# Gated mix of attention and a dense layer on one Trainium2 core: some of VectorE's SBUF-only work handed to GpSimd, W2 loaded in pieces, wider margins behind transfers

## The chip, the cores and the metric

The kernel runs on one core of one Trainium2 chip. The metric is the device time of one execution in microseconds (us), the median of several runs. Lower is better.

## The reference

Softmax attention with 32 heads of width 20 over 2048 positions, and a dense layer with the activation h * tanh(softplus(h)), both from the same x, mixed by a gate per position. Inputs and output are bf16.

```python
def _A_ref(x, wqkv, wo):              # x (1, 2048, 640), wqkv (640, 1920), wo (640, 640)
    H = 32; Dh = 20
    q, k, v = ...                     # (x @ wqkv) split into heads
    scores = jnp.einsum("bhqd,bhkd->bhqk", q, k) * Dh ** -0.5
    o = jnp.einsum("bhqk,bhkd->bhqd", softmax(scores), v)
    return o.reshape(B, S, D) @ wo    # heads side by side

def _B_ref(x, w1, b1, w2):            # w1 (640, 1536), w2 (1536, 640)
    h = x @ w1 + b1
    return (h * jnp.tanh(softplus(h))) @ w2

x = A_x
g = sigmoid((x * gate_w).sum(-1, keepdims=True))
out = g * _A_ref(x, A_wqkv, A_wo) + (1 - g) * _B_ref(x, B_w1, B_b1, B_w2)
```

## The kernel before

**Tiling.** The 2048 queries are four chunks c of 512 columns, the 32 heads eight groups g of four. Within a group each head j has its own 32 partitions of KT and QT, so that four heads' products run beside each other in TensorE's array. The unit of work is a score block (c, g, kt, j): 128 keys by 512 queries of one head, 4 x 8 x 16 x 4 = 2048 of them. TensorE writes a block's scores transposed (keys on partitions) to a PSUM bank (L1149), something takes the exponential, and TensorE multiplies by V with a column of ones in front (L1385), so that row 0 of each head's output O is the sum that normalises it. O of a group gathers in one PSUM bank, ACC.

**Two ways for the exponential.** ScalarE takes most blocks, two or three banks in one activation, into the ring ETS (emit_e, L1176). The others go through VectorE, four heads of one (c, g, kt) as a *tile*: each block is evicted from PSUM as a 16-bit integer, scale times score plus an offset, whose bits read as float16 are about the exponential (emit_x, L1234). To smooth the error, two shifted copies of the tile are made by adding a constant to the integers (piece, L1264, 128 x 2048 int16, SBUF to SBUF; SHADES holds the shifts), and the three patterns are multiplied by V with different weights. GpSimd makes the weighted V, two small instructions of 84 columns for each tile (weigh, L1289), into eight sets of VS. The patterns lie in lines: four of LN, and parts of HB, W2R or REG while these are free. A pattern goes to a spare line, or over the pattern before it once TensorE has read that one. So a tile costs VectorE four evictions and two patterns and spares ScalarE four blocks.

**The planner.** The code does not run loops on the chip; it plans a schedule ahead in Python, and each engine gets its list of instructions in the planned order. Plan.add (L148) books an operation on an engine with a cost: it starts when its engine is free in the plan (pl.now) and its inputs are done. The main loop (L1688 on) goes by steps, one ScalarE activation each: it emits the exponential of a step, composes the scores two steps ahead, decides whether VectorE takes a block (x_block, start_tile), then the products with V (emit_pv), then tasks from a list by due time (pick). Tasks are the projections of Q, K and V, h = x W1 (h_task), the product with W2 (b_task), that of O with Wo (p_task) and the mixing. VectorE's optional work waits in queues: soon (the patterns), blend (the activation's three steps, L968 to L970, on 128 x 1024), norm (the normalisation), bg. work() puts them on VectorE as far as they fit before a given time. An operation that comes from an engine or a transfer counts as safe only its planned end + HOP + RISK of its engine later (safe, L424): 0.5 us for VectorE, 1.2 for transfers and GpSimd.

**The normalisation.** When a group ends (group_done, L1436), VectorE copies ACC to OUNG (L1472); SP sends the four sum rows to RR (L1475, slot nr0); VectorE takes the reciprocal (invert, L1479); SP writes RR to DRAM (L1480) and reads it back spread over the partitions into BCT (L1482, slot nr2); VectorE multiplies OUNG by BCT into QT (times, L1442). This happens 31 times; the last two parts of groups go another way, without transfers. invert and times wait in norm.

**Transfers around it.** All but a few are issued by SP in the planned order. K and Q rows are written to DRAM and read back in the layout with 32 partitions a head (shelve, fetch, row_task, bring; L609, L625, L691, L709), the unused rows of Q being zeroed by clear (L601). W1 comes in blocks of 256 columns (load_w1, L872), W2 in one transfer of all its 1536 rows (load_w2, L878) once its place, W2R, is no longer used for W1 and patterns. Wo follows when the last Q projection is done (load_wo).

The rule by which VectorE picks optional work is the one that the change touches most:

```python
begin = pl.now["dve"]
if op:
    begin = max(begin, op.t1 if op.eng == "dve" and not op.slot else safe(op))
if begin + cost <= until and (best is None or begin < best[0] - 0.01):
    best = (begin, todo, fn)
```

Of the kernel before, what the change touches and what calls it, by code (L numbers as in the profile page):

```python
# [17 lines left out]
P = 128  # L18
# [20 lines left out]
PV_HOLD = 3  # L39
# [7 lines left out]
HOP = 0.1  # L47
# [15 lines left out]
SLACK = 0.22  # L63
LATER = 0.553
THIRD = 0.455
CALLED = 1.926
ROWED = 5
SPARED = 0
KEPT = 8
NEED = 6  # L70
BEFORE = 4
FREE = 0.225
RISK = {"pe": 0.1, "act": 0.3, "dve": 0.5, "pool": 1.2, "sp": 1.2}
AHEAD = 27
BEHIND = 22.677
MORE = 4.131
PATIENCE = 8.798
CATCH_UP = 497.751
BUSY = 0.437
CROWD = 1.357  # L80
MARGIN = 0.475
EAGER = 148
LOAD = 1.055
MISH = 1.7
GROUP = 1.526
LAST = 0
OVER = 0.233
XSLACK = 0.468
BROAD = 1.13
FMIN = 0.109  # L90
VMIN = 1.0
ROOM = 1.319
MORE_MM = 0.005
XBANKS = 2
XLATE = 5.488
# [3 lines left out]
END = 61  # L99
SHIFT = 1.8  # L100
LAG = 394
WINDOW = 3.603
CALM = 10
PACKED = 17
Q_AT = 192
Q_STEP = 17.329
SQ = 36
SQ_STEP = 18
H_AT = 160
H_STEP = 11.375  # L110
# [25 lines left out]
class Plan:  # L136
# [11 lines left out]
    def add(self, eng, fn, deps=(), slot=None, cost=0.1, kind="F", tail=None, bulk=0.0):  # L148
# [87 lines left out]
def bass_gated_mix__softmax_full_mha__dense_activation_mish__prompt_kernel(  # L236
# [123 lines left out]
    def attention(pl, fast):  # L360
# [8 lines left out]
        norm = deque()  # L369
# [54 lines left out]
        def safe(op):  # L424

            return op.t1 + HOP + RISK[op.eng]

        def work(until):
            while True:
# [14 lines left out]
                best[2]()  # L444

# [42 lines left out]
        if fast:  # L488
# [117 lines left out]
            def shelve(name, c, rows, src, ev, n, i=0):  # L606
# [7 lines left out]
                for g, names in k_need.items():  # L614
                    if (g, c) not in k_done and name in names and all((m, c) in k_written for m in names):
                        k_done[(g, c)] = None
                        later(now["step"] + 3, lambda g=g, c=c, names=names: fetch(g, c, names))
# [55 lines left out]
            def row_task(i, c, due):  # L673
# [9 lines left out]
                def finish(bank, last):  # L683
# [8 lines left out]
                    if c not in q_blank:  # L692
# [167 lines left out]
            w2_load = []  # L860
# [16 lines left out]
            def load_w2():  # L877
                w2_load.append(pl.add("sp", lambda e: e.dma_start(  # L878
                    W2, B_w2.rearrange("(f p) c -> p f c", p=P)),
                    [*line_free[("a", 0)], w1_last[FIRST - 2], w1_last[FIRST - 1], *u_free], "w2", cost=0.6, tail=1.7, bulk=9.0))  # L880

            def load_wo():
# [12 lines left out]
                def turn():  # L895

                    if norm or oung_free[0] == "busy":
# [47 lines left out]
            def mish(ev, hb, hc, k):  # L945
# [26 lines left out]
        def b_task(hc, t, half, due):  # L972
# [18 lines left out]
                def ready():  # L991
                    if not gate_done or not w2_load:
# [236 lines left out]
        def emit_x(s, tile, u, bank):  # L1229
# [25 lines left out]
            def piece(n):  # L1255
                def run():
# [4 lines left out]
                    else:  # L1261
                        at, deps = grab()
                    to = line(at)
                    op = pl.add("dve", lambda e: e.tensor_scalar(  # L1264
                        to, src, SHADES[n] - SHADES[held], None, ALU.add), [made, *deps], cost=SHADE)
# [170 lines left out]
        def group_done(c, g, step, last):  # L1436
# [4 lines left out]
            def times(src, deps):  # L1441
                oung_free[0] = bc_read[0] = otn_done[(c, g)] = pl.add("dve", lambda e: e.tensor_tensor(  # L1442
                    otn(c, g), src, BC, ALU.mult), deps, cost=WIDE)

            if end:
                while norm:
                    norm.popleft()[1]()
# [21 lines left out]
            while oung_free[0] == "busy":  # L1469
                norm.popleft()[1]()  # L1470
# [7 lines left out]
            def invert():  # L1478
# [7 lines left out]
                norm.append((WIDE, lambda: times(src, spread), lambda: spread[-1]))  # L1486
# [3 lines left out]
        if fast:  # L1490
# [37 lines left out]
            tasks.sort(key=lambda t: t.due)  # L1528
            later(H_AT - 90, lambda: (load_w1(0), load_w1(1)))
# [160 lines left out]
        while True:  # L1690
# [15 lines left out]
            if fast and area[0] and not w2_load and len(h_done) >= FIRST and line_free[("a", 0)] != "busy":  # L1706
# [34 lines left out]
            while owed > 0:  # L1741
# [9 lines left out]
        assert not queue and not tasks and not bg and not soon and not norm and not tile_now[0] and not blend and not acts, (len(queue), len(tasks), len(bg), len(acts))  # L1751
# [173 lines left out]
```

## Time and profile before

| | |
|---|---|
| median of 3 runs | 775.63 us (770.47 to 776.85) |
| profiled execution | 774.76 us, of which the span is 773.0 |
| busy: ScalarE (ACT) | 745.3 us |
| busy: TensorE (PE) | 735.1 us |
| busy: VectorE (DVE) | 692.5 us |
| busy: GpSimd (POOL) | 154.2 us |
| moved by transfers | 50.42 MB, 65 GB/s in the mean |

In the profile DVE is VectorE, ACT ScalarE, PE TensorE with PEld its weight loads, POOL GpSimd, SPq the issues of SyncE. L1264 is line 1264 of the kernel. A group's row reads: line, engine, operation, output <- inputs (a name is that of the memory, so a pattern in a borrowed line is written REG, W2R or HB), shapes, count | busy time, mean of one in ns | idle time of the engine before it and what ended it. A timeline's row reads: start, length, engine, line, operation, count, and in brackets the idle time before it with what ended it. A wait's row reads: who waited <- for whom: total, times, longest.

### The profile page before, as it was taken

How to read it: one execution, taken by the hardware profiler on the slowest of the kernel's cores; microseconds unless marked ns; L12 is line 12 of the kernel's file. 1: busy time of each engine (PE TensorE's matmuls, PEld its weight loads, DVE VectorE, ACT ScalarE, POOL GpSimd, SP SyncE). 2: the span in 40 equal slices, each digit the busy share in tenths (PEclk: the TensorE clock that was granted, in tenths of full speed). 3: DMA queues.
4: the chain of work that ended last, by engine and by line, in shares of the span. 5: the costliest groups of instructions: out<-in, count | busy, mean ns of one | idle time of the engine just before them, and what ended most of it. 6: DMA issues, size and time to landing. Idle time of an engine off the chain costs nothing.

```text
span 773.0 us, 25310 instructions
## 1 busy us (share of the span) xinstructions
PE 735.1 (95%) x11198; PEld 276.8 (36%) x11203; DVE 692.5 (90%) x1126; ACT 745.3 (96%) x779; POOL 154.2 (20%) x264
## 2 busy tenths in 40 slices
PE   8998998999998998999998999999998999999996
PEld 3333243334323342233333334433433433332333
DVE  3597897989899999879998999999999999999996
ACT  5998998999999999999999999999999999999995
POOL 3213024023212123121121212121222121213210
PEclk9999999999999999999999999999999999999998
DMA  9422221112133332522123111112213122000001
GB/s 227 66 62 63 83 76 31 35 53 74 41 98 106 104 95 74 179 69 54 53 69 97 38 42 52 40 45 65 72 51 85 50 54 63 25 25 16 22 12 45
DMA packets 77836, 50.42 MB, mean 65 GB/s; under 512 B 21232, under 2 KB 73704, under 8 KB 77672
## 3 DMA queue, kind: packets, MB, share of 16 engines
q1 hardware_dynamic: 75352, 48.24, 22.4%
q8 instruction: 91, 1.49, 0.8%
q10 hardware_dynamic: 2256, 0.47, 0.3%
q0 software_dynamic: 112, 0.01, 0.2%
q14 instruction: 25, 0.20, 0.1%
HBM read 39.01 MB, written 8.90 MB: 62 GB/s over the span
## 4 chain that ended last, share of the span: by engine, by line
ACT 77%; PE 14%; DMA 5%; DVE 2%; SPq 1%; issue 0%; ACTq 0%
ACT ETS L1176 74%; PE PS L1149 5%; PE PS L1385 4%; PE PS L455 4%; ACT REG L951 2%; DMA RR<-OUNG 2%; DMA XB<-in_A_x_dram 2%; SPq L504 1%; DMA W2R<-in_B_w_dram 1%; PE PS L799 1%; ACT W2R L951 1%; PE PS L840 0%; DVE HB L1007 0%; DVE LN L1264 0%; DVE LN L1234 0%
## 5 line engine op out<-in xcount | busy, mean ns | idle before, releaser
L1176 ACT ACTIVATE ETS<-PS 128x1024 bf16<-128x1024 f32 (+1 forms) x748 | 723.1, 1191 | 12.2 <-PE PS L1149 10.4
L1149 PE MATMUL PS<-QT,KT 32*128 32x512 bf16 (+1 forms) x2131 | 294.3, 379 | 20.5 <-ACT ETS L1176 16.9
L1234 DVE TENSOR_SCALAR LN<-PS 128x512 int16<-128x512 f32 x368 | 246.5, 680 | 19.5 <-PE PS L1149 18.2
L1289 POOL TENSOR_SCALAR VS<-V_all 128x84 bf16<-128x84 bf16 x250 | 146.8, 587 | 579.6 <-PE PS L1385 404.4
L1149 PEld LDWEIGHTS PS<-QT,KT 32*128 32x128 bf16 x2131 | 72.9, 91 | 248.9 <-ACT ETS L1176 230.6
L1385 PE MATMUL PS<-ETS,V_all 128*21 128x512 bf16 (+1 forms) x1612 | 153.7, 379 | 2.3 <-DVE V_all L809 2.0
L1264 DVE TENSOR_SCALAR LN<-LN 128x2048 int16<-128x2048 int16 x172 | 117.8, 689 | 7.2 <-PE PS L1385 6.3
L455 PE MATMUL PS<-XB,REG 128*32 128x256 bf16 (+1 forms) x1860 | 95.3, 298 | 0.6 <-DMA XB<-in_A_x_dram 0.4
L1385 PE MATMUL PS<-LN,VS 128*21 128x512 f16 (+1 forms) x784 | 73.9, 378 | 1.8 <-DVE LN L1264 1.8
L455 PE MATMUL PS<-W2R,HB 128*32 128x320 bf16 x1536 | 75.4, 301 | 0.1
L1385 PEld LDWEIGHTS PS<-ETS,V_all 128*21 128x21 bf16 x1612 | 39.1, 90 | 62.4 <-issue 51.9
L455 PEld LDWEIGHTS PS<-XB,REG 128*32 128x32 bf16 (+1 forms) x1860 | 43.5, 95 | 27.8 <-issue 15.9
L455 PE MATMUL PS<-WOQ,QT 128*32 128x320 bf16 x1024 | 51.2, 301 | 1.8 <-DVE QT L1465 1.1
L455 PEld LDWEIGHTS PS<-W2R,HB 128*32 128x32 bf16 x1536 | 35.7, 96 | 25.1 <-issue 12.0
L1234 DVE TENSOR_SCALAR REG<-PS 128x512 int16<-128x512 f32 x52 | 35.0, 684 | 2.5 <-PE PS L1149 2.2
L1385 PE MATMUL PS<-LN,V_all 128*21 128x512 f16 (+1 forms) x384 | 36.2, 375 | 0.0
L455 PE MATMUL PS<-XB,WOQ 128*32 128x512 bf16 (+2 forms) x440 | 35.8, 384 | 0.0
L927 DVE TENSOR_TENSOR HB<-PS,B1F 128x512 bf16<-128x512 f32 x48 | 32.6, 679 | 0.1
L1385 PEld LDWEIGHTS PS<-LN,VS 128*21 128x21 bf16 x784 | 18.4, 89 | 38.2 <-issue 23.1
L455 PEld LDWEIGHTS PS<-WOQ,QT 128*32 128x32 bf16 x1024 | 23.5, 96 | 18.1 <-issue 7.9
L1234 DVE TENSOR_SCALAR W2R<-PS 128x512 int16<-128x512 f32 x36 | 24.1, 681 | 3.7 <-PE PS L1149 3.7
L799 PE MATMUL PS<-REG,XB 128*128 128x160 bf16 (+1 forms) x240 | 24.7, 240 | 0.1
(118 smaller groups left out, 508.8 us busy)
## 6 DMA issues: line engine op xcount, KB each, us to landing
REG<-in_B_w_dram SPq DMA_DIRECT2D x36, 320.0 KB, 3.4
BCT<-SUMS SPq DMA_DIRECT2D x31, 256.0 KB
W2R<-in_B_w_dram SPq DMA_DIRECT2D x12, 320.0 KB, 4.8
QT<-QS SPq DMA_DIRECT2D x28, 128.0 KB, 2.3
KT<-KS SPq DMA_DIRECT2D x28, 128.0 KB
KS<-LN SPq DMA_DIRECT2D x16, 128.0 KB, 2.4
QS<-WOQ SPq DMA_DIRECT2D x16, 120.0 KB
W2R<-in_B_w_dram SPq DMA_DIRECT2D x1, 1920.0 KB, 8.4
```

The costliest lines, as they stand in the source:

```text
L455: last = e.matmul(to[at + j:at + j + n, :], w[:, j:j + n], x, start=start, stop=stop, tile_position=(0, at + j))
L504: "sp", lambda e: e.dma_start_transpose(xt(c), x_ap[c * CW:(c + 1) * CW, :]), (), f"xt{c}", cost=4.5)]
L799: return lambda e, bank: e.matmul(PS[:, bank, i * n:(i + 1) * n], xt(t // 4)[:, f, t % 4 * P:(t % 4 + 1) * P], WV[:, f, g * HD:g * HD + n] ...
L927: ev = dve(lambda e: e.tensor_tensor(hb, PS[:, bank, :].rearrange("p (i t) -> p i t", i=2), bias, ALU.add), [last, *b1f, *guarded, *b_read ...
L951: ex = pl.add("act", lambda e: e.activation(U, h, AF.Tanh, bias=MXR[:, 3:4], scale=0.5), [ev, u_free[0], m_bias], cost=0.95)
L1149: op = pl.add("pe", lambda e, to=to, g=real(g), tile=tile, j=j, cols=cols, c=c, of_q=of_q: e.matmul(to[:, cols], KT[32 * j:32 * j + 32, g, ...
L1176: e_op[s] = pl.add("act", lambda e: e.activation(RING[:, p:p + n, :], scores(s)[:, 0:n, :], AF.Exp, scale=SCALE), [s_op[s], *(pv_slot[b] f ...
L1234: bank_free[bank] = x_ops[bank] = tile["op"] = dve(lambda e: e.tensor_scalar(dst, PS[:, bank, :], SCALE * ULPS, BASE, ALU.mult, ALU.add), ...
L1264: op = pl.add("dve", lambda e: e.tensor_scalar(to, src, SHADES[n] - SHADES[held], None, ALU.add), [made, *deps], cost=SHADE)
L1289: weighted[(c, g, k)] = n, [pl.add("pool", lambda e, i=i, n=n, src=src: e.tensor_scalar(VS[:, n, i, :, :], src, WEIGHTS[i + 1], None, ALU. ...
L1385: lasts[n] = pl.add("pe", lambda e, v=v, j=j, src=src[:, cols], of_q=of_q, begin=begin, end=end: e.matmul(PS[32 * j:32 * j + EW, ACC, of_q ...
```

## The change

1. *Patterns on GpSimd.* Plan.add gets an argument port. An operation with port=True starts in the plan no sooner than the last one with port=True ended, on whichever engine. The patterns, the activation's three steps and the product with the reciprocals have it. A new function aid(), called once in each step ahead of work(), takes the first waiting pattern for GpSimd if it can begin there (GpSimd free, no port operation running, input safe) no later than 0.5 us after ScalarE's planned time and at least 0.9 us (AID) before the end of VectorE's booked work. The plan books it there at 1.8 us instead of 0.61. Each pattern now also waits for the pattern made before it of its tile.
2. *The product of O with the reciprocals* (times) goes to GpSimd, all 31, booked at 1.2 us. It waits in a queue of its own, lasting, and is emitted when the transfer into BCT is safe.
3. *Margins.* RISK of transfers goes from 1.2 to 2.2 us, and for the slots nr0 and nr2 it is 4.5 us until 60 steps before the end.
4. *W2 in pieces.* load_w2 books a transfer for each f in range(NFC), 128 rows each, every two steps.
5. *Q's and K's rows.* Reading Q back is booked 7 steps after the write instead of 4 where c > 0; QS is zeroed for c = 2 and 3 at fixed steps, 112 and 136.
6. *Small rules and constants.* An open task is carried on with even when the step's share of task work is used up. PV_HOLD, SPARED, NEED, BEHIND, LOAD, END, Q_AT, H_STEP and others of the planner's constants have other values; these decide when tiles are begun, when tasks are due and how much VectorE may be behind.

```diff
-PV_HOLD = 3
+PV_HOLD = 2
...
-SPARED = 0
+SPARED = 1
 KEPT = 8
-NEED = 6
+NEED = 5
...
+W2_STEP = 2
+K_WAIT = 3
+Q_WAIT = 7
+AID = -0.9
+SHADE_POOL = 1.8
+TIMES = 1.2
-RISK = {"pe": 0.1, "act": 0.3, "dve": 0.5, "pool": 1.2, "sp": 1.2}
+RISK = {"pe": 0.1, "act": 0.3, "dve": 0.5, "pool": 1.2, "sp": 2.2}
-AHEAD = 27
-BEHIND = 22.677
+AHEAD = 24
+BEHIND = 27.779
-LOAD = 1.055
+LOAD = 0.576
-XLATE = 5.488
+XLATE = 8.166
-END = 61
+END = 75
-Q_AT = 192
-Q_STEP = 17.329
+Q_AT = 325
+Q_STEP = 18.125
-H_STEP = 11.375
+H_STEP = 13.632
...
+        if port:
+            at = max(at, self.port)
+            self.port = at + cost
...
         def safe(op):
 
-            return op.t1 + HOP + RISK[op.eng]
+            return op.t1 + HOP + (RISK[op.eng] if op.slot not in ("nr0", "nr2") or now["at"] > NSLOT - 60 else 4.5)
...
+        def aid():
+
+            while soon:
+                op = soon[0][2]()
+                begin = max(pl.now["pool"], pl.port, safe(op))
+                if begin > pl.now["act"] + 0.5 or begin > pl.now["dve"] + AID:
+                    return
+                soon.popleft()[1]("pool")
...
-                            later(now["step"] + 4, lambda g=g: bring(g, c))
+                            later(now["step"] + (Q_WAIT if c else 4), lambda g=g: bring(g, c))
...
             def load_w2():
-                w2_load.append(pl.add("sp", lambda e: e.dma_start(
-                    W2, B_w2.rearrange("(f p) c -> p f c", p=P)),
-                    [*line_free[("a", 0)], w1_last[FIRST - 2], w1_last[FIRST - 1], *u_free], "w2", cost=0.6, tail=1.7, bulk=9.0))
+                deps = [*line_free[("a", 0)], w1_last[FIRST - 2], w1_last[FIRST - 1], *u_free]
+                w2_from.append(now["step"])
+
+                def load(f):
+                    w2_load.append(pl.add("sp", lambda e: e.dma_start(
+                        W2[:, f, :], B_w2[f * P:(f + 1) * P, :]), deps, f"w2{f}", cost=0.5, tail=1.7, bulk=0.8))
+
+                for f in range(NFC):
+                    later(now["step"] + 1 + W2_STEP * f, lambda f=f: load(f))
...
                 def piece(cost, fn, after=None):
                     def run():
-                        last[0] = pl.add("dve", fn, [last[0]], cost=cost)
+                        last[0] = pl.add("dve", fn, [last[0]], cost=cost, port=True)
...
-                    op = pl.add("dve", lambda e: e.tensor_scalar(
-                        to, src, SHADES[n] - SHADES[held], None, ALU.add), [made, *deps], cost=SHADE)
+                    op = pl.add(eng, lambda e: e.tensor_scalar(
+                        to, src, SHADES[n] - SHADES[held], None, ALU.add), [made, tile["items"][-1][0], *deps],
+                        cost=SHADE if eng == "dve" else SHADE_POOL, port=True)
...
             def times(src, deps):
-                oung_free[0] = bc_read[0] = otn_done[(c, g)] = pl.add("dve", lambda e: e.tensor_tensor(
-                    otn(c, g), src, BC, ALU.mult), deps, cost=WIDE)
+                oung_free[0] = bc_read[0] = otn_done[(c, g)] = pl.add("pool", lambda e: e.tensor_tensor(
+                    otn(c, g), src, BC, ALU.mult), deps, cost=TIMES, port=True)
...
-                norm.append((WIDE, lambda: times(src, spread), lambda: spread[-1]))
+                lasting.append((spread[-1], lambda: times(src, spread)))
...
+            if lasting and (safe(lasting[0][0]) < pl.now["act"] or step not in slots):
+                lasting.popleft()[1]()
...
-            while owed > 0:
+            while owed > 0 or now["open"]:
...
+            if fast and busy:
+                aid()
             work(pl.now["act"] + 0.5 if busy else 1e9)
```

More of the change, by code (lines that the diff above doesn't have):

```diff
@@ L146, in __init__, with add @@
         self.queue = 0.0
-    def add(self, eng, fn, deps=(), slot=None, cost=0.1, kind="F", tail=None, bulk=0.0):
+        self.port = 0.0
+    def add(self, eng, fn, deps=(), slot=None, cost=0.1, kind="F", tail=None, bulk=0.0, port=False):
         op = Op(eng, fn, [d for d in deps if d is not None], slot)
@@ L616, in shelve @@
                         k_done[(g, c)] = None
-                        later(now["step"] + 3, lambda g=g, c=c, names=names: fetch(g, c, names))
+                        later(now["step"] + K_WAIT, lambda g=g, c=c, names=names: fetch(g, c, names))
             def fetch(g, c, names):
@@ L691, in finish @@
                         "sp", lambda e: e.dma_start(to, ROWS[n][0:m, :]), [ev], f"qw{n}", cost=0.55, bulk=0.5)
-                    if c not in q_blank:
+                    if c == 1 and c not in q_blank:
                         clear(c)
@@ L895, in turn @@
                 def turn():
-                    if norm or oung_free[0] == "busy":
+                    if norm:
                         later(now["step"] + 1, turn)
@@ L1528, in attention @@
             tasks.sort(key=lambda t: t.due)
+            later(112, lambda: clear(2))
+            later(136, lambda: clear(3))
             later(H_AT - 90, lambda: (load_w1(0), load_w1(1)))
@@ L1705, in attention @@
                 emit_e(step)
-            if fast and area[0] and not w2_load and len(h_done) >= FIRST and line_free[("a", 0)] != "busy":
+            if lasting and (safe(lasting[0][0]) < pl.now["act"] or step not in slots):
+                lasting.popleft()[1]()
+            if fast and area[0] and not w2_from and len(h_done) >= FIRST and line_free[("a", 0)] != "busy":
                 load_w2()
@@ L1749, in attention @@
                 fn()
+            if fast and busy:
+                aid()
             work(pl.now["act"] + 0.5 if busy else 1e9)
-        assert not queue and not tasks and not bg and not soon and not norm and not tile_now[0] and not blend and not acts, (len(queue), len(tasks), len(bg), len(acts))
+        assert not queue and not tasks and not bg and not soon and not norm and not lasting and not tile_now[0] and not blend and not acts, (len(queue), len(tasks), len(bg), len(acts))
         c = NC - 1
```

56 lines of the change are left out of this document (28 added, 28 removed).

## The prediction, made before the result was known

> **What bounds the kernel now.** I read the page's engine rows first, then the groups of ScalarE, then busy time by stage, then ScalarE's own timeline where it stands still.
>
> ```profile
> PE 735.1 (95%) x11198; PEld 276.8 (36%) x11203; DVE 692.5 (90%) x1126; ACT 745.3 (96%) x779; POOL 154.2 (20%) x264
> ACT 77%; PE 14%; DMA 5%; DVE 2%; SPq 1%; issue 0%; ACTq 0%
> L1176 ACT ACTIVATE ETS<-PS 128x1024 bf16<-128x1024 f32 (+1 forms) x748 | 723.1, 1191 | 12.2 <-PE PS L1149 10.4
> L1176 ACT ACTIVATE ETS<-PS 128x1024 bf16<-128x1024 f32 x678 | 643.3, 1152 | 10.7 <-PE PS L1149 8.9 <-PE PS L1385 1.4
> L1176 ACT ACTIVATE ETS<-PS 128x1536 bf16<-128x1536 f32 x69 | 108.3, 1582 | 1.5 <-PE PS L1149 1.5
> L1176 ACT ACTIVATE ETS<-PS 128x512 bf16<-128x512 f32 x1 | 0.6, 594 | 0.0
> ```
>
> ScalarE carries 77% of the chain that ended last. There are 2048 score blocks (4 x 8 x 16 x 4 by the loops); ScalarE takes 678 x 2 + 69 x 3 + 1 = 1564, so VectorE takes 484, which is 121 tiles of four. One block costs ScalarE 723.1 / 1564 = 0.462 us, a tile taken from it 1.85 us. So the time can fall in two ways only: more tiles on VectorE, or fewer waits of ScalarE. TensorE is not the bound in spite of 95%: the row below says that its weight load stands 230.6 us waiting for ScalarE.
>
> ```profile
> 25.00:128.00 103.00, 98.10 (x1213) 35.72 (x1207) 85.53 (x144) 95.77 (x104) 22.92 (x44) 0.97 0.23 64
> 128.00:235.00 107.00, 105.72 (x1387) 37.83 (x1383) 95.87 (x160) 107.00 (x115) 18.80 (x36) 1.00 0.19 57
> 235.00:340.00 105.00, 97.23 (x1334) 34.29 (x1331) 93.32 (x153) 101.33 (x102) 21.90 (x32) 0.98 0.37 108
> 340.00:450.00 110.00, 105.13 (x1748) 39.53 (x1748) 102.80 (x163) 110.00 (x114) 20.76 (x37) 1.00 0.23 60
> 450.00:560.00 110.00, 108.45 (x1901) 43.09 (x1898) 106.34 (x170) 110.00 (x115) 22.20 (x38) 1.00 0.19 54
> 560.00:660.00 100.00, 96.50 (x1693) 38.39 (x1696) 98.27 (x152) 100.00 (x103) 18.94 (x30) 1.00 0.22 60
> 660.00:764.00 104.00, 100.56 (x1695) 37.57 (x1692) 98.47 (x163) 103.68 (x111) 20.42 (x34) 1.00 0.06 19
> ...
> PEld PS L1149 <- ACT ETS L1176: 230.6, 643, 1.3
> ```
>
> Columns: stretch, length, then PE, PEld, DVE, ACT, POOL busy. From 25 to 764 us ScalarE is idle for 739 - 727.8 = 11.2 us only. VectorE is idle for 315 - 274.7 = 40.3 us of the first three stretches and for 424 - 405.9 = 18.1 us (4%) of the last four. After 340 us it is VectorE that limits how many tiles can leave ScalarE; before 340 us it is so only partly.
>
> **GpSimd's added work and VectorE's freed time.**
>
> ```profile
> L1264 DVE TENSOR_SCALAR LN<-LN 128x2048 int16<-128x2048 int16 x172 | 117.8, 689 | 7.2 <-PE PS L1385 6.3 <-issue 0.2
> L1442 DVE TENSOR_TENSOR QT<-OUNG,BCT 128x512 bf16<-128x512 f32 x31 | 21.2, 685 | 0.7 <-DMA BCT<-SUMS 0.7
> L970 DVE SCALAR_TENSOR_TENSOR HB<-REG,U 128x1024 bf16<-128x1024 f32 x18 | 21.9, 1218 | 0.1
> 452.71 0.68 DVE L1264 TENSOR_SCALAR REG<-REG 128x2048 int16<-128x2048 int16 x1
> 453.31 0.68 DVE L1234 TENSOR_SCALAR LN<-PS 128x512 int16<-128x512 f32 x1
> ...
> L1792 POOL TENSOR_TENSOR HB<-LN,W2R 128x320 bf16<-128x320 f32 x1 | 0.9, 857 | 24.4 <-ACT LN L1790 24.4
> L548 POOL COPY WOQ<-WOQ 128x400 bf16<-128x400 bf16 x1 | 0.5, 517 | 4.4 <-DMA WOQ<-in_A_wqkv_dram 4.4
> L562 POOL COPY REG<-GW 128x5 bf16<-128x5 bf16 x1 | 0.2, 204 | 4.7 <-DMA GW<-in_gate_w_dram 4.7
> ```
>
> On VectorE a shifted pattern (L1264) costs 0.60 us of the queue, start to next start (452.71 to 453.31); each tile has two, 242 in all. The product (L1442) counts the same. A tile is four evictions and two patterns, 3.6 us.
>
> On GpSimd no row has a pattern. Its two copies give (517 - 204) / 395 = 0.79 ns an element, so 2048 elements take 0.20 + 1.62 = 1.83 us. The two-input add gives 857 ns for 320, so at most 5.5 us for a pattern at its rate, and 1.25 us for the product of 512 (204 ns held fixed). A pattern has one 16-bit input like the copies: I take 1.83, the low end, and 1.25 for the product.
>
> All 31 products move: 31 x 0.60 = 18.6 us off VectorE. Of the patterns, a number that only the schedule knows: GpSimd takes one when it can begin at least 0.9 us before the end of VectorE's booked work. Bounds: none, and all 242 (242 x 1.83 = 443 us, which fits beside GpSimd's 154). The waits of the next fence put only 13 of the 172 down to TensorE's reading, so most stand behind other VectorE work, but how long they stand is in no row; I take a third, 80, or 48.0 us.
>
> **What comes back through a shared way into SBUF.**
>
> ```profile
> DVE LN L1264 <- PE PS L1385: 6.3, 13, 1.2
> ...
> 129.67 0.92 POOL L1289 TENSOR_SCALAR VS<-V_all 128x84 bf16<-128x84 bf16 x2 [0.32 <-PE PS L1385]
> ...
> 613.78 2.23 POOL L1289 TENSOR_SCALAR VS<-V_all 128x84 bf16<-128x84 bf16 x2 [9.54 <-PE PS L1385]
> ...
> 613.53 1.23 DVE L968 SCALAR_TENSOR_TENSOR REG<-REG 128x1024 f32<-128x1024 f32 x1
> 614.67 0.74 DVE L1264 TENSOR_SCALAR LN<-LN 128x2048 int16<-128x2048 int16 x1
> ```
>
> The same two small GpSimd instructions take 0.92 us in one place and 2.23 us in another, where they begin inside VectorE's L968 and run on through its L1264: GpSimd stood while VectorE worked from SBUF to SBUF. With instructions so short the trace cannot show the reverse, VectorE held by a long GpSimd instruction. At the least it is nothing. At the most, blindly placed: 162 patterns left on VectorE and 72 steps of the activation (24 x 3 by the loops; L970 is one of the three) make 234 such starts in 739 us, 0.317 a us; a 1.83 us instruction meets 0.58 of them, each held half its length, 0.92: 0.53 us a pattern, and by the same 0.25 us a product. The new rule leaves only what runs past 0.9 us of booked work exposed: 0.317 x 0.93 x 0.46 = 0.14 us. The ends are 0.14 and 0.53; the plan's clock and the chip's drift apart, so I take 0.25 throughout, nearer the low end since most VectorE instructions read PSUM: 111 x 0.25 = 28 us back.
>
> The Trainium skill (SBUF — State Buffer, "Who interferes with whom") states that VectorE in a two-port mode or with two SBUF inputs and GpSimd take one port pair as an exclusive lock for a whole instruction, the loser standing fully. The 2.23 us pair agrees for GpSimd as loser; no row has VectorE as loser. It speaks against this change, and blindly placed it would make the time about 766 us.
>
> Net 18.6 + 48.0 - 28 = 38.6 us. Before 340 us (43% of the time) I count half, since VectorE has idle time there: 38.6 x 0.79 = 30.5 us. A tile more costs VectorE 2.4 us of evictions and 0.8 us for the patterns left to it, and its 1.85 us of shorter span takes 0.92 x 1.85 = 1.7 us of VectorE's time away: 4.9 us. So 6.2 tiles more, and 6.2 x 1.85 = **11.5 us** off ScalarE.
>
> **Wider margins, W2 and the moved steps.**
>
> ```profile
> 72.98 1.02 ACT L1176 ACTIVATE ETS<-PS 128x1024 bf16<-128x1024 f32 x1 [2.06 <-PE PS L1149]
> ...
> 124.38 1.02 ACT L1176 ACTIVATE ETS<-PS 128x1024 bf16<-128x1024 f32 x1 [2.29 <-PE PS L1149]
> 126.70 2.10 ACT L1176 ACTIVATE ETS<-PS 128x1024 bf16<-128x1024 f32 x2 [1.29 <-PE PS L1149]
> ...
> 252.07 1.45 ACT L1176 ACTIVATE ETS<-PS 128x1536 bf16<-128x1536 f32 x1 [1.50 <-PE PS L1149]
> ...
> 70.48 0.25 DVE L1479 RECIPROCAL RR<-RR 128x16 f32<-128x16 f32 x1 [2.31 <-DMA RR<-OUNG]
> ...
> 122.08 0.25 DVE L1479 RECIPROCAL RR<-RR 128x16 f32<-128x16 f32 x1 [3.19 <-DMA RR<-OUNG]
> ...
> 250.75 0.95 PE L455 MATMUL PS<-XB,W2R 128*32 128x256 bf16 x28 [1.67 <-DMA W2R<-in_B_w_dram]
> ...
> W2R<-in_B_w_dram SPq DMA_DIRECT2D x1, 1920.0 KB, 8.4
> ```
>
> Four idle stretches, 2.06 + 2.29 + 1.29 + 1.50 = 7.1 us of ScalarE's 11.2, follow a transfer that landed later than planned: VectorE sat at the reciprocal for 2.31 and 3.19 us with evictions queued behind it, and TensorE at a W1 block for 1.67. The margin for the reciprocal's transfers goes from 1.2 to 4.5 us, 3.3 more, over both waits: 5.6 us go. The others go from 1.2 to 2.2: 1.0 of 1.67, 0.9 us. Together **6.5 us**. Late next is the product, now on GpSimd behind BCT<-SUMS; the weighted values queued behind it there have SETS = 8 buffers made ahead. The normalisation's chain grows by at most 2 x 3.3 us; a group lasts 739 / 32 = 23 us and covers it; without that cover the copy out of ACC would be held, up to 6.6 us a group.
>
> W2 as one transfer lands in 8.4 us and no ScalarE wait follows it; the pieces (the loop makes twelve, one per 128 rows, every two steps) add eleven issues on SP and bring the last one some 22 us later. The first product with W2 waits for all, but has h tasks and scores to run beside: zero; at worst TensorE's b tasks move 22 us and press on the end, a few us. Zeroing QS for c = 2, 3 earlier and reading QS three steps later lie on SP beside running groups: zero, at worst one wait of the kind seen above, 2 us. The Q projections, now due from step 325 on, leave the stage with 40.3 us of idle VectorE and load the one with 18.1: at worst 2 us each way. The other constants alter only which ready work is chosen: zero, within the range.
>
> New: a pattern on GpSimd is ready 1.2 us later, and the weighted values queue behind it; TensorE has 230.6 us of waiting to hide this, but the last product of a group does not wait gracefully. I add **3 us** (0 to 8).
>
> **Sum.** -11.5 - 6.5 + 3 = -15.0. The profiled execution took 774.76 us (span 773.0 and 1.8 around it), 0.9 below the median of three, 775.63. 774.8 - 15.0 = 759.8, so 760.
>
> **Rivals.**
> *The hold decides (slower).* Place: L1264 on VectorE behind a GpSimd pattern of the same tile, which it now also waits for by the added dependency. Price: if a GpSimd instruction holds VectorE for 1.0 us instead of 0.25, that is 83 us, 47 of them after 340 us; 18 fall into idle time and 29 land on ScalarE, whose blocks the plan has already given away: 760 + 29 = 789. It passes 774.8 when 15 land, 33 us after 340, 58 in all: at 0.77 us an instruction. For it: the 2.23 us pair and VectorE's 96%. Against: the schedule books the two apart, and evictions read PSUM. The skill's lock, cited above, is this mechanism. Chance 0.23.
> *It does not do what it says.* GpSimd finds VectorE seldom booked 0.9 us ahead and takes 15 patterns: 18.6 + 9 - 12 = 15.6, x 0.79 / 4.9 = 2.5 tiles, 4.6 us; and the margins only move the stalls, so 6.5 becomes 1: 774.8 - 5.6 + 1 = 770. For it: 96% busy leaves short queues when evictions follow TensorE; against: the first stretches show waits that a margin can meet. Chance 0.15.
> *More goes over.* 160 patterns: 96 + 18.6 - 48 = 66.6, x 0.79 = 52.6; a tile then costs 2.4 + 0.4 + 1.7 = 4.5, so 11.7 tiles, 21.6 us; with 5 us of late patterns, 774.8 - 21.6 - 6.5 + 5 = 752. For it: a larger backlog is now allowed before a tile is refused. Chance 0.12.
>
> **How the numbers follow.** The forecast, 750 to 767, has 0.50. Faster by over 1% (about what a measurement here can tell from no change) is the forecast and the third rival, 0.62; within 1% is the second, 0.15; slower is the first, 0.23. The range runs from 744 (third rival with its late patterns at nothing and some more tiles) to 790, the first rival at 1.0 us.
>
> **What would show it.** Right: L1264 with POOL as engine, about 80 of 242 or more, 1.8 us each; L1442's product on POOL near 1.25 us; evictions at L1234 up from 484 to about 508; ScalarE's blocks down to about 1540; no wait of 2 us at the reciprocal; ScalarE's idle from 25 us on below 8 us. Wrong: L1264 or the activation's steps on VectorE well over 0.69 and 1.22 us in their mean, ScalarE idle behind TensorE behind VectorE after 340 us, or patterns on GpSimd of 3 us and more.

## The result and the profile after

The changed kernel takes 1097.86 us (median of 4 runs, 1093.03 to 1100.71) against 775.75 for the kernel before: 1.417 times as long, 95% interval 1.411 to 1.423. The prediction was 760, with 744 to 790 as its range.

The page of the changed kernel: engines, the chain that ended last, and the groups that answer to those shown before (ScalarE's blocks are now L1201, the patterns L1289, the product L1468, the activation's last step L995).

```profile
PE 870.5 (80%) x11243; PEld 295.6 (27%) x11243; DVE 835.9 (76%) x1053; ACT 759.6 (69%) x782; POOL 718.2 (66%) x407
PEclk9977976788678678968998888887988889888889
POOL 39%; PE 38%; DVE 17%; issue 2%; ACT 2%; DMA 1%; SPq 1%; POOLq 0%; DVEq 0%
L1201 ACT ACTIVATE ETS<-PS 128x1024 bf16<-128x1024 f32 (+1 forms) x751 | 732.5, 1056 | 300.8 <-PE PS L1174 297.9
L1289 POOL TENSOR_SCALAR LN<-LN 128x2048 int16<-128x2048 int16 x63 | 343.9, 5459 | 166.6 <-PE PS L1411 105.6
L1289 DVE TENSOR_SCALAR LN<-LN 128x2048 int16<-128x2048 int16 x108 | 152.7, 1414 | 42.0 <-POOL LN L1289 20.2
L1468 POOL TENSOR_TENSOR QT<-OUNG,BCT 128x512 bf16<-128x512 f32 x31 | 40.9, 1320 | 73.7 <-DMA BCT<-SUMS 66.9
L995 DVE SCALAR_TENSOR_TENSOR HB<-REG,U 128x1024 bf16<-128x1024 f32 x18 | 45.1, 2504 | 0.0
```

GpSimd heads the chain with 39%, where ScalarE had 77%. ScalarE stands 300.8 us, and 297.9 of that end with TensorE's scores. A pattern takes 5.45 us in the mean on GpSimd (96 of them over all lines of memory, 83 of them 5.37), booked at 1.8. VectorE's own patterns, 0.69 us before, take 1.41 in the mean (those of the row shown), the activation's step 2.50 instead of 1.22, though nothing in these instructions changed. The eviction from PSUM keeps its 0.68 us. TensorE's granted clock, 9 tenths in every slice but the last before, now falls to 6 in some; over the execution it is 0.84 where it was 0.99, and TensorE is busy for 80% of the span instead of 95%. No run here parts the lower clock from what came first, so what it adds to the loss stays open.

The waits of the changed kernel, the first and those of TensorE for GpSimd (total, times, longest; the waits of PE lie within those of its weight loads, PEld, so they do not add up; over all lines of memory TensorE stands 178 us for GpSimd's patterns):

```profile
ACT ETS L1201 <- PE PS L1174: 297.9, 215, 8.5
PEld PS L1411 <- POOL LN L1289: 140.9, 54, 4.8
PE PS L1411 <- POOL LN L1289: 123.2, 51, 4.5
```

One place of the timeline, each engine's rows of the same stretch (start, length):

```profile
590.04 5.37 POOL L1289 TENSOR_SCALAR LN<-REG 128x2048 int16<-128x2048 int16 x1
...
590.11 5.84 DVE L1289 TENSOR_SCALAR LN<-LN 128x2048 int16<-128x2048 int16 x1 [4.01 <-POOL LN L1289]
595.88 0.67 DVE L1259 TENSOR_SCALAR LN<-PS 128x512 int16<-128x512 f32 x1
...
590.13 0.40 PE L1411 MATMUL PS<-LN,VS 128*21 128x512 f16 x4 [3.03 <-POOL LN L1289]
590.36 1.40 PE L474 MATMUL PS<-WOQ,QT 128*32 128x320 bf16 x36
591.68 0.39 PE L1174 MATMUL PS<-QT,KT 32*128 32x512 bf16 x2
596.61 0.60 PE L1174 MATMUL PS<-QT,KT 32*128 32x512 bf16 x1 [4.54 <-DVE LN L1259]
...
592.11 1.02 ACT L1201 ACTIVATE ETS<-PS 128x1024 bf16<-128x1024 f32 x1 [2.85 <-PE PS L1174]
599.18 2.10 ACT L1201 ACTIVATE ETS<-PS 128x1024 bf16<-128x1024 f32 x2 [6.04 <-PE PS L1174]
...
615.63 5.37 POOL L1289 TENSOR_SCALAR LN<-LN 128x2048 int16<-128x2048 int16 x1
...
615.89 4.46 DVE L995 SCALAR_TENSOR_TENSOR HB<-REG,U 128x1024 bf16<-128x1024 f32 x1
```

The place shows two ways in which the long pattern costs time. First it is late: until 590.1 TensorE stands 3.03 us and VectorE 4.01 us for the GpSimd pattern that ended then (VectorE's own pattern is of the same tile and now has to wait for it). The scores come further on in TensorE's list, at 591.68, and ScalarE has then stood idle for 2.85 us. Then it holds VectorE: VectorE starts its own pattern 0.07 us after GpSimd has begun another, and that instruction of 0.68 us takes 5.84; it ends 0.54 us after GpSimd's. The eviction behind it in VectorE's list, which reads PSUM, starts at 595.88 only. TensorE's next scores wait 4.54 us for that eviction, and ScalarE stands idle for 6.04 us. The step at 615.89 is held too, but ends 0.65 us *ahead* of GpSimd's end. The trace of before could not show either.

### The profile page after: what moved, and what is told of

Same layout as the page of the kernel before. It is cut to its first block, busy times and chain, and to the rows that moved or that the text cites. A ratio compares the mean times of both kernels' runs of the same rounds, so it can differ in the third digit from the quotient of the medians.

```text
span 1094.0 us, 25427 instructions
## 1 busy us (share of the span) xinstructions
PE 870.5 (80%) x11243; PEld 295.6 (27%) x11243; DVE 835.9 (76%) x1053; ACT 759.6 (69%) x782; POOL 718.2 (66%) x407
## 3 DMA queue, kind: packets, MB, share of 16 engines
q8 instruction: 90, 1.47, 0.5%
## 4 chain that ended last, share of the span: by engine, by line
POOL 39%; PE 38%; DVE 17%; issue 2%; ACT 2%; DMA 1%; SPq 1%; POOLq 0%; DVEq 0%
POOL LN L1289 27%; PE PS L1411 14%; PE PS L1174 11%; PE PS L474 10%; DVE LN L1289 5%; DVE LN L1259 4%; POOL REG L1289 4%; POOL W2R L1289 3%; ACT ETS L1201 2%; POOL VS L1315 2%; POOL HB L1289 2%; DVE HB L995 2%; DVE REG L993 2%; DMA XB<-in_A_x_dram 1%; PE PS L818 1%
## 5 line engine op out<-in xcount | busy, mean ns | idle before, releaser
L1201 ACT ACTIVATE ETS<-PS 128x1024 bf16<-128x1024 f32 (+1 forms) x751 | 732.5, 1056 | 300.8 <-PE PS L1174 297.9
L1289 POOL TENSOR_SCALAR LN<-LN 128x2048 int16<-128x2048 int16 x63 | 343.9, 5459 | 166.6 <-PE PS L1411 105.6
L1174 PE MATMUL PS<-QT,KT 32*128 32x512 bf16 (+1 forms) x2116 | 334.0, 427 | 19.9 <-DVE LN L1259 8.8
L1259 DVE TENSOR_SCALAR LN<-PS 128x512 int16<-128x512 f32 x396 | 265.7, 683 | 98.1 <-PE PS L1174 96.1
L1289 DVE TENSOR_SCALAR LN<-LN 128x2048 int16<-128x2048 int16 x108 | 152.7, 1414 | 42.0 <-POOL LN L1289 20.2
L1411 PE MATMUL PS<-ETS,V_all 128*21 128x512 bf16 (+1 forms) x1580 | 172.8, 434 | 0.3 <-DVE V_all L799 0.3
L474 PE MATMUL PS<-XB,REG 128*32 128x256 bf16 (+2 forms) x1860 | 105.7, 330 | 0.9 <-DVE LN L1259 0.7
L1468 POOL TENSOR_TENSOR QT<-OUNG,BCT 128x512 bf16<-128x512 f32 x31 | 40.9, 1320 | 73.7 <-DMA BCT<-SUMS 66.9
L474 PEld LDWEIGHTS PS<-XB,REG 128*32 128x32 bf16 (+1 forms) x1860 | 47.1, 103 | 33.9 <-issue 22.4
L1289 POOL TENSOR_SCALAR LN<-W2R 128x2048 int16<-128x2048 int16 x7 | 37.6, 5370 | 25.1 <-DVE W2R L1259 24.9
L1289 POOL TENSOR_SCALAR REG<-LN 128x2048 int16<-128x2048 int16 x8 | 43.8, 5477 | 6.9 <-DVE LN L1259 3.4
L995 DVE SCALAR_TENSOR_TENSOR HB<-REG,U 128x1024 bf16<-128x1024 f32 x18 | 45.1, 2504 | 0.0
```

The source lines that it names most:

```text
L474: last = e.matmul(to[at + j:at + j + n, :], w[:, j:j + n], x, start=start, stop=stop, tile_position=(0, at + j))
L995: piece(BROAD, lambda e: e.scalar_tensor_tensor(h, U, c, G, ALU.add, ALU.mult), done)
L1174: op = pl.add("pe", lambda e, to=to, g=real(g), tile=tile, j=j, cols=cols, c=c, of_q=of_q: e.matmul(to[:, cols], KT[32 * j:32 * j + 32, g, ...
L1201: e_op[s] = pl.add("act", lambda e: e.activation(RING[:, p:p + n, :], scores(s)[:, 0:n, :], AF.Exp, scale=SCALE), [s_op[s], *(pv_slot[b] f ...
L1259: bank_free[bank] = x_ops[bank] = tile["op"] = dve(lambda e: e.tensor_scalar(dst, PS[:, bank, :], SCALE * ULPS, BASE, ALU.mult, ALU.add), ...
L1289: op = pl.add(eng, lambda e: e.tensor_scalar(to, src, SHADES[n] - SHADES[held], None, ALU.add), [made, tile["items"][-1][0], *deps], cost= ...
```

## Experiments

Theory A: the pattern's length on GpSimd, 5.4 us for 1.8 booked, makes the loss, in two ways: TensorE stands for late patterns, VectorE is held. Rival B: the other constants and moved steps. Rival C: GpSimd's hold on SBUF ruins the schedule at any length. Each ratio is against runs of the kernel before that were made beside it; the brackets are 95% intervals.

**No patterns on GpSimd.**

```diff
-            if fast and busy:
-                aid()
```

> The changed kernel with the one call of aid() taken out, so that VectorE makes all patterns; the products stay on GpSimd, and margins, W2 in pieces and all constants stay. Theory A (the pattern on GpSimd takes 5.37 us where the plan books 1.8, and all of the loss comes from that): near the kernel before, 755 to 790 us, and ScalarE's idle from 25 us on below 20 us. Rival B (the other constants and the moved tasks bring a good part of the loss): 850 us or more.

783.87 us, 1.010 times the kernel before (1.005 to 1.016). The loss is in aid(); the rest is not worth a gain. ScalarE's waits are as before, but the end is later. TensorE's last long row here, and its last but one in the kernel before:

```profile
764.51 11.35 PE L474 MATMUL PS<-WOQ,QT 128*32 128x320 bf16 x312
```

```profile
764.65 0.83 PE L455 MATMUL PS<-WOQ,QT 128*32 128x320 bf16 x16 [0.25 <-issue]
```

312 matmuls of O x Wo are left over in one row when ScalarE has finished, where before it was 16: tasks that now come later no longer fit beside the blocks. Whether the new due times, the margins or other constants move them is not told apart here.

**The same plan with patterns cut to the booked length.**

```diff
-                        to, src, SHADES[n] - SHADES[held], None, ALU.add), ...
+                        to[:, :, 0:w], src[:, :, 0:w], ...   # w = 160 on GpSimd, CW on VectorE
```

> The changed kernel with the same plan, but a pattern that GpSimd makes covers 160 of each head's 512 columns, 640 elements instead of 2048; the other columns of that pattern are left as they were (work left out). At the 2.52 ns an element of the long ones that is 0.2 + 1.6 = 1.8 us, what the plan books. Theory A: the time that the plan was made for, 750 to 785 us, as my sum had it with 1.83 us; patterns on VectorE near 0.7 us, no TensorE wait for GpSimd over 1 us. Rival C (GpSimd's hold on SBUF hurts at any length): 830 us or more.

765.46 us, 0.988 (0.983 to 0.993). Three rows: GpSimd's patterns, VectorE's patterns, ScalarE's wait.

```profile
L1290 POOL TENSOR_SCALAR LN<-LN 128x640 int16<-128x640 int16 x63 | 123.3, 1958 | 153.9 <-PE PS L1412 106.9 <-DVE LN L1290 17.6 <-DVE LN L1259 13.1
...
L1290 DVE TENSOR_SCALAR LN<-LN 128x2048 int16<-128x2048 int16 x108 | 80.8, 748 | 9.6 <-PE PS L1412 6.2 <-POOL LN L1290 2.1 <-DVE W2R L1290 0.7
...
ACT ETS L1201 <- PE PS L1174: 9.2, 11, 3.4
```

With the length that the plan believes in, the same order of work takes 332 us less than the changed kernel. B falls, and so does C for a pattern of this length; A stands.

**The right length in the plan.** SHADE_POOL = 5.4 instead of 1.8.

> The changed kernel with SHADE_POOL = 5.4 instead of 1.8, so that the plan books what the chip takes; it will give GpSimd fewer patterns and keep VectorE's SBUF work away from them. Theory A in the form that the wrong booking is what hurts: 770 to 850 us, waits of TensorE for patterns of GpSimd small. If a 5.4 us pattern on GpSimd hurts even when booked rightly: 900 us or more.

884.38 us, 1.139 (1.133 to 1.146), between the two cases and in neither. GpSimd still gets 51 patterns, tiles fall from 130 to 100 (400 evictions), and VectorE's patterns of LN still take 1.105 us in the mean:

```profile
L1289 DVE TENSOR_SCALAR LN<-LN 128x2048 int16<-128x2048 int16 x102 | 112.7, 1105 | 26.9 <-PE PS L1411 18.4 <-POOL LN L1289 7.6
```

The port rule keeps VectorE's SBUF work away from GpSimd's in the plan, yet on the chip VectorE's patterns and steps are still lengthened by 88 us in sum. Against the kernel before, ScalarE has 84 blocks more (39 us), waits 43 us more for scores, and the stretch after its last block is 11 us longer: 93 of the 107 us. Booking rightly makes an instruction of 5.4 us bearable, not useful.

**The two ways apart.** First the hold without the lateness: TensorE reads old values of KT where a pattern of GpSimd is due.

```diff
+                    was = [op]
+                    if op.eng == "pool":
+                        src = KT[:, 0, :].bitcast(F16).rearrange("p (j t) -> p j t", t=CW)
+                        was = [k_done[(0, i)] for i in range(NC)]
...
-                        line_free[at] = [lasts[HG - 1]]
+                        line_free[at] = [lasts[HG - 1], op]
```

> The changed kernel in which TensorE does not use GpSimd's patterns: where one is due it multiplies values of KT that have long been there, so it waits for none of them; GpSimd still makes each one in full, 5.37 us, and the line is given back only after both (the output then lacks these patterns). Tells the two ways apart in which a long pattern can hurt. Late patterns alone (TensorE, in order, stands waiting for them): below 850 us. Hold alone (VectorE stands while GpSimd reads and writes SBUF): 1000 us or more. By the profile's sums, some 170 us of TensorE's waits for GpSimd and some 174 us of lengthened VectorE instructions, both: about 930 us.

1027.74 us, 1.326 (1.319 to 1.334), as the hold alone had it. TensorE waits for no pattern of GpSimd here. Some lateness is left: 32 us in which TensorE waits for the weighted V, which GpSimd makes behind the patterns, and 37 us in which VectorE waits for patterns. Then the lateness without the long hold: cut patterns behind 36 tiny memsets.

```diff
+                        for _ in range(36 if eng == "pool" else 0):
+                            spent[0] += 1
+                            e.memset(SC[:, spent[0] % 1184:spent[0] % 1184 + 1], 0)
+                        return e.tensor_scalar(
+                            to[:, :, 0:w], src[:, :, 0:w], ...)   # w = 160 on GpSimd
```

> The changed kernel with GpSimd's patterns cut to 160 of 512 columns (1.8 us, work left out) and 36 one-element memsets of some 98 ns ahead of each, so that a pattern is ready after about 5.4 us as in the change, but holds SBUF for 1.8 us only. Lateness without the long hold, the counterpart of the unwaited run. If the two add up: 765 + 70 = 835 us. If lateness alone would already do most of it, the unwaited run having lost time for another reason: 950 us or more.

806.05 us, 1.038 (1.034 to 1.043), in neither case. But this run is not as late as it was meant to be. One pattern of it on GpSimd:

```profile
596.01 1.10 POOL L1296 MEMSET SC<- 128x1 uint8 x36
597.18 1.81 POOL L1297 TENSOR_SCALAR LN<-LN 128x640 int16<-128x640 int16 x1
```

A memset lasts 0.10 us, but the next starts 0.03 us after it, so all 36 take 1.1 us and not 3.5. A pattern is ready 2.97 us (median) after the first memset starts, 1.2 us later than in the cut run, where the change's are 3.6 us later. The rows of the unwaited run, then of the late one:

```profile
L995 DVE SCALAR_TENSOR_TENSOR HB<-REG,U 128x1024 bf16<-128x1024 f32 x18 | 47.9, 2662 | 0.0
...
ACT ETS L1201 <- PE PS L1174: 228.6, 160, 9.1
...
PEld PS L1415 <- DVE LN L1289: 99.1, 47, 6.4
```

```profile
L997 DVE SCALAR_TENSOR_TENSOR HB<-REG,U 128x1024 bf16<-128x1024 f32 x18 | 22.8, 1268 | 0.0
...
ACT ETS L1203 <- PE PS L1176: 41.6, 58, 5.1
PEld PS L1421 <- POOL LN L1297: 37.9, 42, 2.4
```

Against the cut patterns' 765 us the unwaited run loses 262 of the 332 us. Even if the 32 and 37 us of lateness left in it counted in full, some 190 us would remain (an estimate, and with a granted clock of 0.87 in it): VectorE's being held is enough for most of the loss. TensorE's waits for patterns add the other 70 us. The late run loses 41 us for a third of the change's lateness. What the whole lateness costs without the hold no run shows; in proportion it would be some 125 us (an estimate: 41 x 3.56 / 1.16), more than those 70, so the two would overlap and do not simply add. The list of waits alone misleads: it puts 178 us on TensorE standing for GpSimd's patterns in the changed kernel and only 34 on VectorE, since a held instruction counts as busy.

**aid() alone on the kernel before.**

> The kernel before with aid() alone: patterns may go to GpSimd, booked at 1.8 us, with the port rule and the added dependency; products, margins, W2 and all constants as before. Theory A: the pattern's length does it without the rest, 1000 to 1150 us. Rival B (the other constants make it so bad): below 900 us.

1123.24 us, 1.448 (1.438 to 1.457): it needs none of the other edits; 113 patterns went to GpSimd.

**A length between.** 320 of 512 columns.

> The changed kernel with the same plan and GpSimd's patterns cut to 320 of each head's 512 columns, 1280 elements (work left out): 0.2 + 3.2 = 3.4 us by the long ones, between the 1.8 of 640 and the 5.4 of 2048. If the loss grows straight with the time over the booked one: 765 + 333 x 1.6 / 3.6 = 915 us. If it grows with its square, since the exposed part both meets more VectorE work and holds each longer: 765 + 333 x 0.2 = 832 us.

902.72 us, 1.165 (1.157 to 1.172), near the 915. The patterns took 3.45 us, and the loss grows about straight with the time over the booked one.

**Products back on VectorE,** without aid().

> The changed kernel without aid() and with the products back on VectorE; margins, W2 in pieces and constants stay. If what the no-aid run lost against the kernel before (1%, with a tail of O x Wo after the last exponential) comes from the moved tasks and constants: 780 to 800 us, the tail still there. If it came from GpSimd's products: 770 to 778 us.

794.59 us, 1.024 (1.017 to 1.031), with 236 matmuls of O x Wo left at the end in one row: the constants and moved tasks cost it, not the products, and the products on GpSimd are worth some 10 us beside these constants. Two plans differ in more than the edit, so that difference is not a pure price.

**The wider margins alone** on the kernel before.

> The kernel before with the wider margins alone (2.2 us for transfers, 4.5 us for nr0 and nr2). My term of 6.5 us holds: 765 to 771 us and no VectorE wait over 1 us at the reciprocal. Rival (the stalls move to other places and the later normalisation costs as much): 772 to 785 us, ScalarE's idle from 25 us on still above 9 us.

815.23 us, 1.050 (1.046 to 1.055), outside both cases. ScalarE's waits in the body and the one at the end:

```profile
ACT LN L1790 <- PE PS L455: 39.1, 1, 39.1
ACT ETS L1176 <- PE PS L1149: 10.6, 13, 3.2
```

VectorE's waits at the reciprocal are gone as forecast (6.8 us in four before, none here), but in the body ScalarE gains nothing by it: 10.6 us in 13 waits, 10.4 in 12 before. The loss is the tail, where a wait of 39 us was 3.1 before: the plan decides everything anew, and with these margins and the old due times TensorE's tasks came out late.

**A shorter way to make a whole pattern.** Two 16-bit values as one 32-bit integer, added to a constant pair by a two-input integer add. Booked at 2.4 us, then at 1.8 (the change's own plan), then that on the kernel before.

```diff
+                    src32, to32 = src.bitcast(I32), to.bitcast(I32)
+                    c32 = SH[:, i, :].bitcast(I32).unsqueeze(2).to_broadcast([P, HG, CW // 2])
...
+                        ... if eng == "dve" else (lambda e: e.tensor_tensor(
+                        to32, src32, c32, ALU.add)), ...
```

> The changed kernel with another way to make a pattern on GpSimd: the 16-bit values taken two at a time as 1024 32-bit integers and added to a constant pair by a two-input integer add (the constant of the upper half is one lower, for the carry), booked at 2.4 us. At the product's (1272 - 205) / 512 = 2.08 ns an element that is 0.2 + 2.1 = 2.3 us. Theory A (the length of the pattern is all that is wrong): 755 to 785 us. Rival C (any hold of SBUF by GpSimd above 2 us is ruinous here): over 830 us.

> The changed kernel with GpSimd's patterns made by the 32-bit integer add, which took 1.89 us in the run before, and booked at 1.8 us as in the change, so that the plan is the change's own. Theory A: what the run with the cut patterns gave, 762 to 770 us, but with whole patterns: faster than both kernels by 1% over the one before. Rival (a whole pattern hurts where a cut one does not): above 785 us.

> The kernel before with aid() alone as in the earlier run, patterns of GpSimd made by the 32-bit add (1.89 us) and booked at 1.8 us; constants, products and margins as before. If freeing VectorE is what counts: 755 to 768 us. If the constants of the change are needed for it: 772 to 795 us.

790.08 us, 1.017 (1.010 to 1.024); 784.40 us, 1.011 (1.007 to 1.014); 813.48 us, 1.049 (1.045 to 1.053). A whole pattern takes 1.89 us, a third of the 16-bit way, and yet the second run has 19 us more than the cut patterns of 1.81 us with the same plan. All three lie above what I expected of theory A (the second just under its rival's 785 us, the third above both of its cases), and on the old constants, which send 113 patterns to GpSimd, the loss is largest. The step L999 of this run and L995 of the cut one, the same instruction of the same place:

```profile
L999 DVE SCALAR_TENSOR_TENSOR HB<-REG,U 128x1024 bf16<-128x1024 f32 x18 | 30.4, 1691 | 0.0
```

```profile
L995 DVE SCALAR_TENSOR_TENSOR HB<-REG,U 128x1024 bf16<-128x1024 f32 x18 | 23.8, 1320 | 0.0
```

So VectorE is held more by an instruction that is hardly longer. Theory D: what counts is the time for which GpSimd holds SBUF. Theory E: the 0.08 us by which it is longer than the cut pattern. Two runs with work left out tell: the 16-bit add on 168 columns (1.90 us), and the 32-bit add on 160.

> As the run with cut patterns, but 168 of 512 columns instead of 160 (work left out): by 2.52 ns an element 1.90 us, the length of the 32-bit add in the run that took 784 us, with the same plan. In the traces a pattern made by the 16-bit add lets VectorE go at fixed points, the first some 1.2 us before its end, the 32-bit one only 0.13 us before it. Theory D (what counts is how long SBUF is held, not how long the instruction takes): 763 to 771 us. Theory E (0.08 us more than booked is what sets the plan off): 778 to 790 us.

> As the run with the 32-bit add booked at 1.8 us, same plan, but of 160 of 512 columns, 320 integers (work left out): 0.2 + 320 x 1.65 ns = 0.73 us, held to its end. Theory D: little hold is left, 755 to 768 us. If something else in that kernel cost the 19 us (its four added memsets, another order): 778 us or more.

765.12 us, 0.987 (0.984 to 0.991), and 763.77 us, 0.985 (0.982 to 0.989). E falls: the same length with a shorter hold costs nothing (the activation's 72 steps take 1.27 us in the mean, 1.54 with the whole 32-bit add), and the other kernel with patterns of 0.72 us is as fast.

Last, whole patterns in pieces, each a shorter hold.

```diff
+                        for j in range(0, HG, 1):     # 2 for the halves
+                            last = e.tensor_tensor(to32[:, j:j + 1, :], src32[:, j:j + 1, :], c32, ALU.add)
```

> The changed kernel's plan with whole patterns: the 32-bit add of a pattern made head by head, four instructions of 256 integers, each 0.2 + 256 x 1.65 ns = 0.63 us, 2.5 us in all against the booked 1.8. VectorE can get in between two of them, so a hold lasts 0.63 us at most instead of 1.89. Theory D (length of a hold): hold down to a third of the 39 us, lateness 0.6 us a pattern up: 764 to 775 us, faster than the kernel before by up to 1%. Theory E (all time over the booked one hurts, held or not): 790 us or more.

> The same in two instructions of 512 integers, each 0.2 + 512 x 1.65 ns = 1.05 us, 2.1 us in all. Theory D: between the quarters and the whole (784 us), 768 to 779 us. Theory E: 785 to 795 us.

787.71 us, 1.015 (1.012 to 1.017), above what theory D gave and near the 790 of E, and 775.92 us, 1.000 (0.997 to 1.003), within D's range. GpSimd's pieces and TensorE's wait for them, of the quarters and of the halves:

```profile
L1301 POOL TENSOR_TENSOR LN<-LN,SH 128x256 int32<-128x256 int32 x252 | 176.4, 730 | 118.5 <-PE PS L1425 80.6 <-DVE LN L1299 15.7 <-DVE LN L1263 11.1
...
PEld PS L1425 <- POOL LN L1301: 24.1, 31, 1.8
```

```profile
L1301 POOL TENSOR_TENSOR LN<-LN,SH 128x512 int32<-128x512 int32 x126 | 146.2, 1180 | 132.8 <-PE PS L1425 99.0 <-DVE LN L1299 16.2 <-DVE REG L1299 7.3
...
PEld PS L1425 <- POOL LN L1301: 7.5, 17, 1.2
```

The halves gain 8 us on the whole add and equal the kernel before. The quarters hold least (the 72 steps take 1.32 us in the mean, 1.47 with the halves, 1.54 with the whole), but their pattern takes 2.8 us from the first piece's start to the last one's end, 1 us over the booked time. The late run above lost 41 us by 1.2 us of lateness with little hold, so lateness of this size is enough for the 22 us that the quarters lose against the cut patterns. Both lengths count; no whole version beat the kernel before.

## Why the prediction was wrong, step by step

**The step that failed is the price of a pattern on GpSimd:** "I take 1.83, the low end". It takes 5.37 us. The copies that I took it from are another operation. The instruction of the same kind was in my own fence: two VS multiplications of 84 columns in 0.92 us, 0.42 each in the trace's median. With the fixed 0.204 us of the five-element copy, that is 0.213 / 84 = 2.54 ns an element, and 0.2 + 2048 x 2.54 ns = 5.4 us, what was measured. I named 5.5 as the upper end, and then did not carry it into the range.

**The rival that ends slower had the right place and mechanism.** VectorE held at L1289, behind and beside a GpSimd pattern, was the first rival, passing break-even at 0.77 us an instruction. Over all 164 patterns left to it (1.35 us in the mean instead of 0.69) and 72 steps (2.14 instead of 1.21), VectorE is held 108 + 67 = 175 us, 1.4 us for each of the 127 instructions. I had sized it with 1.83 us, hence 0.25. The 3 us for late patterns rested on the same length: TensorE stood 178 us for them. The exclusive lock of the Trainium skill (SBUF — State Buffer, "Who interferes with whom") is borne out with VectorE as loser. That the loser stands for the whole instruction is not quite so here: a step goes on 1.87 us before the end of GpSimd's pattern of 5.37.

**With the booked length the total comes near, in part by luck.** In the cut run 96 patterns moved (80 taken), tiles rose by 9 (6.2), ScalarE's blocks fell from 1564 to 1528, 36 x 0.462 = 16.6 us (11.5), the product took 1.28 us in the median and 1.34 in the mean (1.25), and the whole gained 10 to 12 us (15). The larger gain on ScalarE made up for two terms that failed, the margins and the end (both below). And even this flatters the sum: these patterns let VectorE go early. Whole ones of 1.89 us lost 8 us against the kernel before.

**A held VectorE was priced too low** even so. I exchanged its time for tiles at 1.85 / 4.9, 0.38 us for each. That is right for time that the plan knows of. What the plan does not know of comes after the tiles are given away, and costs nearly the whole: from the cut run to the whole 32-bit one VectorE's patterns and steps are lengthened by some 24 us, and ScalarE's idle between its first and last block, beyond back-to-back issue (0.904 us for two banks, 1.330 for three, 1.039 for an activation of h), rose by 43.0 - 22.4 = 20.6 us, the time by 19.

**The margins' 6.5 us did not come.** By themselves they removed the waits at the reciprocal, but ScalarE's waiting in the body stayed the same. **The moved steps were not zero:** from ScalarE's last block to the end of the span it was 9.1 us before, 14.6 in the cut run and 18.7 without aid(), by left-over O x Wo; I had put zero, at worst a few. **The products** took about the length that was predicted.

## What to carry to other kernels

Price an instruction on another engine from the trace's nearest row of the same operation, with the fixed part taken off by its shortest instruction, not from a cheaper relative; and carry the upper end into the range when a factor of three lies between the ends. Before GpSimd takes work from SBUF beside a saturated VectorE, ask how long one instruction holds SBUF against it: the hold does not show as a wait but as longer VectorE instructions, and it falls on whoever was promised VectorE's time. Look in the trace whether an added delay has the length that it was meant to have. In a planned schedule a new margin or constant is not a local edit: judge it by the whole plan, its end included.

## What the hardware showed beyond expectation

- GpSimd's tensor-scalar costs 2.52 ns an element, for bf16 and int16 alike ((5371 - 417) / 1964); its 32-bit integer add of two inputs 1.65 ns ((1892 - 205) / 1024), its fp32 product 2.08, its bf16 copy 0.79.
- A VectorE pattern that starts early in a whole GpSimd pattern ends at GpSimd's end + 0.54 us, as if it had begun 0.14 us before that end (all 27 in the changed kernel). A step with two inputs from SBUF goes on earlier: 1.87 us before the end of the 16-bit add of 2048 elements, 0.59 before that of 1280 and 1.23 before that of 640, but only 0.13 us before the end of the 32-bit add. Why is open; only the times are shown.
- Evictions from PSUM were held by none of this: 0.68 us in the mean of every run, 0.70 at the longest.
- GpSimd's memsets of one element last 0.10 us each, but follow one another every 0.03 us.
